# Side matmuls in column tiles, an end stage in halves and other constants in a fused attention kernel's written order

## The chip, the core and the metric

The kernel runs on one core of a Trainium2 chip. The metric is the device time of one execution in microseconds; smaller is better. The engines named below are TensorE (PE in the profile, with PEld for its weight loads), ScalarE (ACT), VectorE (DVE), GpSimd (POOL) and SyncE (SP), whose queue here only starts DMAs.

## What is computed

One block with layer norm, 32-head attention over 2048 tokens of 640 features (20 per head), and a gated linear unit whose output scales the attention's:

```python
def _A_ref(x, wqkv, wo):          # H = 32, Dh = 20
    q, k, v = heads of x @ wqkv
    p = _softmax(einsum("bhqd,bhkd->bhqk", q, k) * Dh ** -0.5)
    return (einsum("bhqk,bhkd->bhqd", p, v) as [B, S, D]) @ wo

def _B_ref(x, w_gate, w_up, w_down):          # F = 1728
    h = _sigmoid(x @ w_gate) * (x @ w_up)
    return h @ w_down

xn = _layernorm(x)
s = _A_ref(xn, A_wqkv, A_wo)
g = _silu(_B_ref(xn, B_w_gate, B_w_up, B_w_down))
return x + s * g
```

The inputs are bf16.

## The kernel before, in words

**Blocks and tiles.** Heads go in 8 groups of 4, queries in 4 chunks of 512: 32 blocks. A block has 64 score tiles of 128 keys by 512 queries, one for each of 16 key tiles and 4 heads. The last two head groups alternate (`gc_of`), so block 30 is group 6 and block 31 group 7 of the last chunk, and blocks 28 and 29 are those of the third.

**The three kinds of TensorE work.** Scores (`score_mm`, L883) use tiles of 32 rows by 128 columns, up to four at a time (one for each head). PV (`pv_emit`, L920) uses tiles of 128 rows by 21 columns at columns 0, 32, 64 and 96, four at a time, which add into one bank, `oacc`. Everything else is a side item: query, key and value projections, gate and up (`mk_gu`, L677), down (`mk_down`, L723) and output rows (`mk_out`, L778). These use the whole array, 128 by 128, except for the bound of the later groups (`mk_bu`, L601), which writes four tiles of 6 columns.

**The exponential is shared.** ScalarE takes two score tiles in one instruction (`pt`) and now and then a third (`px`). VectorE takes one tile at a time out of PSUM as bits (`iv`, L1264) and makes the exponential of four such tiles in three passes (L998, L1001, L1004 into `pb`).

**The order is written out.** A loop with a clock of its own (`now`, in steps of 0.02 us) walks through the work before anything runs and puts each instruction into its engine's program as soon as that engine, a bank and the buffers are free by its table of durations: `T_F`, `T_PV`, `T_MM` 0.2133 us, `T_MODE` 0.107 for a change between kinds, `EL` and `PL` for the way of a result. Each round of scores (`nxt = "F"`) fills one half of ScalarE's PSUM (`scA`) and perhaps a bank more for ScalarE and one for VectorE. `URGENT`, `WAIT3`, `DQ`, `STARVE` decide when a round comes and how many tiles it takes; `D_LAST_END` is the number of tiles left in the last block at which VectorE takes no more. The chip then runs each engine's program in that order and waits on semaphores.

**Normalization of a block.** `norm_a` copies `oacc` to `on` and sends the denominators through DRAM into `lt`; 6.5 us later by the table `norm_b` takes the reciprocal (L959) and sends it back, spread over rows, as `rl`. From 7.2 us after that GpSimd multiplies in four parts (L969), each placed by `beat` behind a PSUM read of VectorE. `norm_c` then starts four or five copies into `oU` at once (L988). `o_at[b]`, 4.8 us later, opens what reads them: the output rows of a chunk wait for the block in `need` (block 29 for the third chunk, eight items).

**The end.** When the last PV is out, `chain` takes block 31 another way: two copies of `oacc` (`e_on`, L1036), transposes (L1040), division (`div_scale`, L751 and L753), transposes back (L1050) and copies into `oU` (L1053). The last chunk's product with `wo` is made in advance for the four row tiles of features that don't need block 31: `fill` holds one matmul of 512 columns (`mains`) and one of 128 (`rest`) per row tile and feature tile `kd` 0 to 3 (L1025). `kd` 3 needs block 30. Those in banks 0 to 2 start only once no item is left and at most `FILL_AT` tiles are unclaimed. The fifth feature tile (`late_mm`, L1029) and the elementwise work and output (`tail_steps`, L1077 to L1102) come after `chain`.

Of the kernel before, what the change touches and what calls it, by code (L numbers as in the profile page):

```python
# [18 lines left out]
P = 128  # L19
# [32 lines left out]
def kernel(  # L52
# [393 lines left out]
    T_IV, T_ON = 0.605, 0.60  # L446
    T_PASS = (0.1333, 0.1333, 0.27)
# [21 lines left out]

    class Item:  # L470
        def __init__(self, ops, at, need=None, pre=(), gates=None):
# [26 lines left out]
    def k_mm1(ps, g, c, kd):  # L498
        nc.tensor.matmul(ps, lhsT=wslice(g, 1, kd), rhs=xnT[:, c, kd, :],
                         start=(kd == 0), stop=(kd == KD - 1))  # L500

    def mk_q(b, at):
# [6 lines left out]
        def mm(kd):  # L509
            nc.tensor.matmul(st["ps"], lhsT=wslice(g, 0, kd), rhs=xnT[:, c, kd, :],  # L510
                             start=(kd == 0), stop=(kd == KD - 1))
# [4 lines left out]
        def ev():  # L516
# [3 lines left out]
                     ("PE", None, [(T_MM, lambda: q_bound(st["ps"], g, st["aq"]))]),  # L520
# [14 lines left out]
    def u_mm(st, u, i, c, kd):  # L535
        nc.tensor.matmul(st["ps"], lhsT=wus[u][:, kd, i, :], rhs=xnT[:, c, kd, :],  # L536
                         start=(kd == 0), stop=(kd == KD - 1))

    def mk_ku(u, c, at):
# [5 lines left out]
        def ev():  # L545
            st["k"] = wk.tile([P, QC], BF16, tag="ku", bufs=2, name="ku")[0:UC, :]
# [26 lines left out]
    def mk_qu(u, c, at):  # L573
# [10 lines left out]
        def ev():  # L584
            st["q"] = wk.tile([P, QC], BF16, tag="ku", bufs=2, name="qu")[0:UC, :]
# [7 lines left out]
    def mk_bu(u, at):  # L593
# [10 lines left out]
        def ev():  # L604
            bt = wk.tile([P, QC], BF16, tag="ku", bufs=2, name="bt")
# [4 lines left out]
        return Item([("PE", alloc, [(T_MM + 2 * T_MODE, mm)]),  # L610
# [30 lines left out]
    def mk_v(pr, tts, at):  # L641
# [10 lines left out]
        def done(t):  # L652
            for tt in tts:
                v_at[(pr, tt)] = t
        return Item([("PE", alloc, [(0.08, lambda i=i, kd=kd: mm(i, kd)) for i in range(len(tts)) for kd in range(KD)]),
                     ("DVE", 0.065 + 0.167 * len(tts), lambda: v_evac(st["ps"], pr, tts), "free", done)], at)

    def mk_gu(c, kf, at):
# [16 lines left out]
        def mm(key, i, kd):  # L675
            w = wgu_tiles[(c, k2)]
            nc.tensor.matmul(st[key][0:fs, :], lhsT=w[:, i, kd, ko * P:ko * P + fs],  # L677
                             rhs=xnT[:, c, kd, :], start=(kd == 0), stop=(kd == KD - 1))
# [9 lines left out]
        def mm2(kd):  # L688
            nc.tensor.matmul(st["g"], lhsT=wgu_tiles[(c, k2)][:, 0, kd, P:2 * P],
                             rhs=xnT[:, c, kd, :], start=(kd == 0), stop=(kd == KD - 1))  # L690
# [24 lines left out]
    def mk_down(c, t4, h, at):  # L715
# [6 lines left out]
        def mm(kf):  # L722
            nc.tensor.matmul(st["ps"][:, 0:HD], lhsT=hT[:, kf, t4 * P:(t4 + 1) * P],  # L723
                             rhs=wd[:, kf, h * HD:(h + 1) * HD],
                             start=(kf == 0), stop=(kf == NFT - 1))
# [40 lines left out]
    def mk_out(tt, h, at):  # L766
# [9 lines left out]
        def mm(kd):  # L776
            hs = slice(h * HD, (h + 1) * HD)
            nc.tensor.matmul(st["ps"][:, 0:HD], lhsT=oU[:, kd, tt * P:(tt + 1) * P], rhs=wo[:, kd, hs],  # L778
                             start=(kd == 0), stop=(kd == KD - 1))
# [176 lines left out]
    def norm_b(b, on, lt):  # L956
# [10 lines left out]
        def part(i):  # L967
            cs = slice(i * P, (i + 1) * P)
            ins = nc.gpsimd.tensor_tensor(out=on_bf[:, cs], in0=on[:, cs], in1=rl[:, cs], op=ALU.mult)  # L969
            if i == QC // P - 1:  # L970
                norm_c(b, on_bf)
                o_at[b] = now + 4.8
            return ins
        for i in range(QC // P):
            pool_q.append((now + 7.2, "n", lambda i=i: part(i)))

    def norm_c(b, on_bf):
        g, c = gc_of(b)
        for j in range(GH):
# [3 lines left out]
            while left:  # L983
# [4 lines left out]
                nc.sync.dma_start(out=oU[o:o + m, t, c * QC:(c + 1) * QC], in_=on_bf[r:r + m, :])  # L988
                f += m
                r += m  # L990
                left -= m

# [27 lines left out]
    mains = [scA[1][:, 0, :], scA[1][:, 1, :], bank[0], bank[1]]  # L1020
# [13 lines left out]
    def e_on(i):  # L1034
        last["on", i] = w2.tile([P, QC], FP32, tag="on", bufs=2, name="on")[:, 0:HQ]
# [16 lines left out]
    def e_o(i):  # L1052
        nc.vector.tensor_copy(out=oU[0:GC, KD - 1, c0 + i * HQ:c0 + (i + 1) * HQ], in_=last["t", i][0:GC, 0:HQ])  # L1053

    chain = [("DVE", 0.34, lambda: e_on(0), ()), ("DVE", 0.34, lambda: e_on(1), ()),
             ("PE", 0.40, lambda: e_tr(0), (0,)), ("PE", 0.40, lambda: e_tr(1), (1,)),
             ("DVE", 0.50, lambda: e_scale(0), (2, 3)), ("DVE", 0.50, lambda: e_scale(1), (2, 3)),
             ("PE", 0.25, lambda: e_back(0), (4,)), ("PE", 0.25, lambda: e_back(1), (4, 5)),
             ("DVE", 0.27, lambda: e_o(0), (6,)), ("DVE", 0.27, lambda: e_o(1), (7,))]
    chain_end = {}  # L1060

    def chain_next(eng):
        k = next((k for k, x in enumerate(chain) if x[0] == eng and k not in chain_end), None)
        return k if k is not None and all(chain_end.get(d, 1e9) <= now for d in chain[k][3]) else None

    def chain_run(k):
# [4 lines left out]
    fill = [(t4 - 2, 0.2133, lambda t4=t4, kd=kd: early(mains[t4], t4, slice(0, 512), kd))  # L1071
            for t4 in (2, 3, 0, 1) for kd in range(KD - 1)]
    fill[2 * (KD - 1):2 * (KD - 1)] = [
        (2, 0.07, lambda t4=t4, kd=kd: early(rest[:, t4 * EX:(t4 + 1) * EX], t4, slice(512, D), kd, t4 == 0))
        for t4 in range(4) for kd in range(KD - 1)]

    def tail_steps():  # L1077
        tmps = [hfl[:, t4 * 2 * D:t4 * 2 * D + 1024].bitcast(FP32) for t4 in range(4)]
        xg = xl.rearrange("p (t u) -> p t u", u=D)
        tmp = hfl[:, 8 * D:8 * D + 8 * EX].bitcast(FP32).rearrange("p (t e) -> p t e", e=EX)  # L1080
# [384 lines left out]
```

## Time and profile before

| | us |
|---|---|
| median of 3 runs | 814.01 |
| lowest and highest | 813.37, 815.41 |
| profiled execution, its own time | 813.36 |
| its span, first to last instruction | 811.6 |
| TensorE, VectorE, ScalarE busy | 776.3, 774.6, 780.8 |
| GpSimd busy | 107.7 |
| HBM traffic over the span | 69 GB/s |

A row of the page gives line, engine, operation, output and input, shape and count, then busy time, the mean of one in ns, and the idle time before. A row of the timeline gives start and duration in us. Several matmuls of one group start within some ns of each other and each is listed with its own full latency, so what a group costs is read from start to start, not from its duration. The granted TensorE clock is 0.995 over the span.

### The profile page before, as it was taken

What the parts mean: (1) busy time and instruction counts of PE and PEld (TensorE: products, weight loads), DVE (VectorE), ACT (ScalarE), POOL (GpSimd) and SP (SyncE); (2) the same over time, 40 slices, a digit from 0 to 9 for tenths busy, and PEclk for the clock granted to TensorE, in tenths of its full rate; (3) what the DMA queues carried; (4) which work ended last, traced back from release to release, by engine and by line L of the source; (5) the groups of instructions that cost most, each with busy time, mean ns of one, the idle gap of its engine ahead of it and who ended that gap; (6) DMA issues with size and microseconds to landing.
All of it is one profiled execution on the core that took longest, in us unless ns stands there. A gap on an engine that the chain in (4) does not pass through costs nothing. (4 is left out here: it accounts for less than half of the span.)

```text
span 811.6 us, 17415 instructions
## 1 busy us (share of the span) xinstructions
PE 776.3 (96%) x6480; PEld 273.2 (34%) x6480; DVE 774.6 (95%) x1248; ACT 780.8 (96%) x991; POOL 107.7 (13%) x225
## 2 busy tenths in 40 slices
PE   7899999999999999999999999999999999999995
PEld 5522222333333323333333222333333223333332
DVE  7799999999999999999999999999999999999995
ACT  8899999999999999999999999999999999999991
POOL 7200000000010000000000000000100203203124
PEclk9999999999999999999999999999999999999998
DMA  5531211123222223212112131232222232312211
GB/s 160 156 103 50 66 52 40 59 58 96 63 70 69 68 58 85 66 55 61 55 58 67 51 100 54 71 104 81 63 70 60 72 88 67 123 57 82 83 52 61
DMA packets 91797, 59.96 MB, mean 74 GB/s; under 512 B 34868, under 2 KB 85604, under 8 KB 91712
## 3 DMA queue, kind: packets, MB, share of 16 engines
q1 hardware_dynamic: 91424, 58.52, 25.8%
q8 instruction: 51, 0.84, 0.4%
q14 instruction: 34, 0.28, 0.1%
q10 hardware_dynamic: 288, 0.33, 0.1%
HBM read 45.18 MB, written 11.09 MB: 69 GB/s over the span
## 5 line engine op out<-in xcount | busy, mean ns | idle before, releaser
L82 ACT ACTIVATE pt<-scA 128x1024 bf16<-128x1024 f32 x704 | 694.7, 1142 | 4.1 <-PE bk L883 3.1
L1264 DVE TENSOR_SCALAR iv<-bk 128x512 int16<-128x512 f32 x504 | 333.6, 681 | 10.2 <-PE bk L883 9.0
L883 PE MATMUL scA<-q,kT 32*128 32x512 bf16 x1401 | 273.1, 382 | 12.9 <-ACT pt L82 7.7
L883 PE MATMUL bk<-q,kT 32*128 32x512 bf16 x647 | 207.4, 383 | 0.1
L920 PE MATMUL oacc<-pt,v 128*21 128x512 bf16 x1401 | 179.4, 382 | 0.6 <-DVE on L949 0.6
L883 PEld LDWEIGHTS <-kT 32*128 32x128 bf16 x2048 | 84.1, 91 | 260.5 <-issue 249.6
L920 PE MATMUL oacc<-pb,v 128*21 128x512 bf16 x1008 | 159.7, 382 | 0.8 <-DVE pb L1004 0.7
L1004 DVE TENSOR_TENSOR pb<-iv,pb 128x2048 bf16<-128x2048 bf16 x126 | 153.9, 1221 | 1.0
L677 PE MATMUL bk<-xnT,wgu 128*128 128x512 bf16 x520 | 148.0, 383 | 1.6 <-DVE iv L1264 0.7
L969 POOL TENSOR_TENSOR on_bf<-on,rl 128x128 bf16<-128x128 f32 x124 | 59.3, 481 | 636.2 <-DVE pb L1004 160.1
L82 ACT ACTIVATE px<-bk 128x512 bf16<-128x512 f32 x143 | 100.5, 717 | 2.7 <-POOL hT L1113 1.6
L998 DVE TENSOR_SCALAR pb<-iv 128x2048 int16<-128x2048 int16 x126 | 86.3, 685 | 0.9
L1001 DVE TENSOR_SCALAR pb<-iv 128x2048 int16<-128x2048 int16 x126 | 86.9, 690 | 0.1
L723 PE MATMUL bk<-wd,hT 128*128 128x320 bf16 x448 | 83.8, 302 | 2.2 <-DVE iv L1264 1.4
L920 PEld LDWEIGHTS <-v 128*21 128x21 bf16 x2552 | 49.4, 91 | 86.4 <-issue 63.5
L677 PEld LDWEIGHTS <-wgu 128*128 128x128 bf16 x520 | 38.2, 97 | 67.6 <-issue 47.9
L920 PE MATMUL oacc<-px,v 128*21 128x512 bf16 x143 | 49.0, 382 | 0.0
L723 PEld LDWEIGHTS <-hT 128*128 128x128 bf16 x448 | 34.6, 97 | 41.4 <-issue 33.8
L536 PE MATMUL bk<-xnT,wu 128*128 128x512 bf16 x160 | 47.3, 383 | 1.2 <-DVE qu L586 1.0
L82 ACT ACTIVATE tnh<-bk 128x512 bf16<-128x512 f32 (+1 forms) x56 | 39.7, 709 | 0.1
L685 DVE SCALAR_TENSOR_TENSOR hT<-tnh,bk 128x512 bf16<-128x512 bf16 x52 | 35.3, 679 | 1.4 <-PE bk L677 0.7
L794 POOL TENSOR_TENSOR xnT<-otmp,xnT 128x160 bf16<-128x160 f32 x48 | 26.2, 567 | 47.9 <-DVE pb L1001 15.6
(111 smaller groups left out, 408.2 us busy)
## 6 DMA issues: line engine op xcount, KB each, us to landing
rl<-rd SPq DMA_DIRECT2D x124, 64.0 KB
wgu<-in_B_w_gate_dram SPq DMA_DIRECT2D x24, 320.0 KB
wgu<-in_B_w_up_dram SPq DMA_DIRECT2D x24, 320.0 KB
gq_dram<-gqs SPq DMA_DIRECT2D x24, 160.0 KB
xnT<-gq_dram SPq DMA_DIRECT2D x12, 320.0 KB
xt<-in_A_x_dram SPq DMA_DIRECT2D x16, 160.0 KB
xnT<-in_A_x_dram SPq DMA_DIRECT2D x16, 160.0 KB
out_dram<-xnT SPq DMA_DIRECT2D x14, 160.0 KB
```

The source lines that it names most:

```text
L82: return nc.scalar.add_instruction(mybir.InstActivation(func=func, name=nc.get_next_instruction_name(), engine=ENG.Activation, ins=[nc.sca ...
L536: nc.tensor.matmul(st["ps"], lhsT=wus[u][:, kd, i, :], rhs=xnT[:, c, kd, :], start=(kd == 0), stop=(kd == KD - 1))
L677: nc.tensor.matmul(st[key][0:fs, :], lhsT=w[:, i, kd, ko * P:ko * P + fs], rhs=xnT[:, c, kd, :], start=(kd == 0), stop=(kd == KD - 1))
L685: return nc.vector.scalar_tensor_tensor(out=hT[0:fs, kf, :], in0=st["t"][0:fs, :], scalar=1.0, in1=st["u"][0:fs, :], op0=ALU.add, op1=ALU. ...
L723: nc.tensor.matmul(st["ps"][:, 0:HD], lhsT=hT[:, kf, t4 * P:(t4 + 1) * P], rhs=wd[:, kf, h * HD:(h + 1) * HD], start=(kf == 0), stop=(kf = ...
L883: nc.tensor.matmul(dst, lhsT=kTs[gc_of(b)[0] % 2][32 * j:32 * j + 32, kt * P:(kt + 1) * P], rhs=qts[b % 3][32 * j:32 * j + 32, :], start=T ...
L920: nc.tensor.matmul(oacc[32 * j:32 * j + DH + 1, :], lhsT=lhsT, rhs=u["src"], start=first, stop=last, tile_position=(0, 32 * j), skip_group ...
L969: ins = nc.gpsimd.tensor_tensor(out=on_bf[:, cs], in0=on[:, cs], in1=rl[:, cs], op=ALU.mult)
L998: ins = nc.vector.tensor_scalar(out=pb[:, 0, :, :].bitcast(I16), in0=iv, scalar1=0x7F80, scalar2=1, op0=ALU.bitwise_and, op1=ALU.bitwise_or)
L1001: ins = nc.vector.tensor_scalar(out=pb[:, 1, :, :].bitcast(I16), in0=iv, scalar1=0x007F, scalar2=0x3F00, op0=ALU.bitwise_and, op1=ALU.bitw ...
L1004: ins = nc.vector.tensor_tensor(out=pb[:, 1, :, :], in0=iv.bitcast(BF16), in1=pb[:, 1, :, :], op=ALU.mult)
L1264: beat(nc.vector.tensor_scalar(out=d["iv"][:, j, :], in0=bank[bk], scalar1=B_OFF, scalar2=0.0, op0=ALU.add, op1=ALU.max))
```

## The change

- All side matmuls except those of the value projection go through `cols`: four matmuls of 32 columns of weights, at PV's four column positions, in place of one of 128. The order's table counts PV and these as one family (`FAM`), the value projection and the end's matmuls as another (`full`, "W").
- The bound item is counted without its two changes.
- `norm_b` comes 9.0 us after `norm_a` (`T_LT`) for all blocks but block 30, which keeps 6.5.
- Block 30's multiply is one instruction (`whole`), placed 6.5 us after its reciprocal, not behind reads of VectorE. In the last block `beat` also lets other GpSimd work go that is 1 us late (`LATE`).
- The copies into `oU` are started 1.5 us apart (`T_OU`) for all blocks but the last two, and `o_at` is later by as much.
- The end: the two copies of `oacc` share one buffer; banks 0 and 1 serve row tiles 0 and 1, `scA[1]` row tiles 2 and 3; `kd` 3 waits for block 30 by the table, the others don't; the late matmuls, elementwise work and output become steps of `chain` in two halves, so the second half's transposes can lie beside the first half's work. The sequence of elementwise steps on VectorE stays.
- `ku` gets a third buffer. `URGENT` 0.15 to 0.2, `D_LAST_END` 12 to 20, `WAIT3` 0 to 0.2, `DQ` 1.0 to 1.4, `STARVE` 0.2 to 0.3, `FILL_AT` 24 to 40.

```diff
-URGENT, ROUNDS, HOLD, SLACK, LEAD, LAG, D_LAST, D_LAST_END = 0.15, 6, 0.0, 0.0, 40.0, 2.0, 20, 12
-M_ORD, WAIT3, FALL, M_END = 1, 0.0, 1, 2.0
+URGENT, ROUNDS, HOLD, SLACK, LEAD, LAG, D_LAST, D_LAST_END = 0.2, 6, 0.0, 0.0, 40.0, 2.0, 20, 20
+M_ORD, WAIT3, FALL, M_END = 1, 0.2, 1, 2.0
...
-XMAX, DQ, DORD, XORD, STARVE = 2, 1.0, 2, 0, 0.2
+XMAX, DQ, DORD, XORD, STARVE = 2, 1.4, 2, 0, 0.3
-FILL_AT = 24
+FILL_AT = 40
...
+    LATE, T_LT, T_OU = 1.0, 9.0, 1.5
...
+    def cols(out, lhsT, rhs, start, stop):
+        for j in range(0, P, 32):
+            nc.tensor.matmul(out[j:j + 32, :], lhsT=lhsT[:, j:j + 32], rhs=rhs, start=start, stop=stop,
+                             tile_position=(0, j), skip_group_check=True)
+
+    FAM = {"F": 0, "PV": 1, "M": 1, "W": 2, None: 3}
...
-            nc.tensor.matmul(st["ps"][:, 0:HD], lhsT=hT[:, kf, t4 * P:(t4 + 1) * P],
-                             rhs=wd[:, kf, h * HD:(h + 1) * HD],
-                             start=(kf == 0), stop=(kf == NFT - 1))
+            cols(st["ps"][:, 0:HD], hT[:, kf, t4 * P:(t4 + 1) * P], wd[:, kf, h * HD:(h + 1) * HD],
+                 kf == 0, kf == NFT - 1)
...
-        if psum and prev is not None and x is not None and pool_at[0] <= now + 0.1:
+        if x is not None and base() == NBLK - 1 and x[0] + LATE <= now and pool_at[0] <= now:
+            pool_q.remove(x)
+            x[2]()
+            pool_at[0] = now + 0.5
+        elif psum and prev is not None and x is not None and pool_at[0] <= now + 0.1:
...
+        def whole():
+            nc.gpsimd.tensor_tensor(out=on_bf, in0=on, in1=rl, op=ALU.mult)
+            norm_c(b, on_bf)
+        if b == NBLK - 2:
+            timed.append((now + 6.5, whole))
+            return
...
-                nc.sync.dma_start(out=oU[o:o + m, t, c * QC:(c + 1) * QC], in_=on_bf[r:r + m, :])
+                parts.append((oU[o:o + m, t, c * QC:(c + 1) * QC], on_bf[r:r + m, :]))
...
+        for i, (o, x) in enumerate(parts):
+            if b < NBLK - 2:
+                timed.append((now + T_OU * i, lambda o=o, x=x: nc.sync.dma_start(out=o, in_=x)))
+            else:
+                nc.sync.dma_start(out=o, in_=x)
+        o_at[b] = now + 4.8 + (T_OU * (len(parts) - 1) if b < NBLK - 2 else 0.0)
...
-    mains = [scA[1][:, 0, :], scA[1][:, 1, :], bank[0], bank[1]]
+    mains = [bank[0], bank[1], scA[1][:, 0, :], scA[1][:, 1, :]]
...
     def e_on(i):
-        last["on", i] = w2.tile([P, QC], FP32, tag="on", bufs=2, name="on")[:, 0:HQ]
+        if i == 0:
+            last["on"] = w2.tile([P, QC], FP32, tag="on", bufs=2, name="on")
+        last["on", i] = last["on"][:, i * HQ:(i + 1) * HQ]
...
              ("DVE", 0.27, lambda: e_o(0), (6,)), ("DVE", 0.27, lambda: e_o(1), (7,)),
+             ("PE", 0.54, lambda: e_late(0), (8,), (0, 1)),
+             ("DVE", 0.63, lambda: t_main(0), (10,)), ("DVE", 0.63, lambda: t_main(1), (10,)),
+             ("DVE", 0.9, lambda: t_done(0), (10,)),
+             ("PE", 0.54, lambda: e_late(1), (9,), (0, 1, 2, 3)),
+             ("DVE", 0.63, lambda: t_main(2), (14,)), ("DVE", 0.63, lambda: t_main(3), (14,)),
+             ("DVE", 1.6, lambda: t_done(1), (14,))]
...
+    fill = fills(lambda t: t, (0, 1), pre, *main) + fills(lambda t: 2, (0, 1), pre, *narrow)
+    fill += fills(lambda t: t, (0, 1), [KD - 2], *main) + fills(lambda t: 2, (0, 1), [KD - 2], *narrow)
+    fill += fills(lambda t: t + 1, (2, 3), pre, *main) + fills(lambda t: 2, (2, 3), pre, *narrow)
+    fill += fills(lambda t: t + 1, (2, 3), [KD - 2], *main) + fills(lambda t: 2, (2, 3), [KD - 2], *narrow)
...
+            if kd == KD - 2 and o_at.get(NBLK - 2, 1e9) > now:
+                return False
...
-                        end = now + T_F + (T_MODE if mode != "F" else 0.0)
+                        end = now + T_F + (T_MODE if fam != "F" else 0.0)
...
-                    dur = T_PV + (T_MODE if mode != "PV" else 0.0)
+                    dur = T_PV + (T_MODE if FAM[fam] != 1 else 0.0)
```

`t_main`, `t_rest`, `t_last` and `t_out` hold the elementwise work and the output DMAs of the former `tail_steps`, cut by row tile; `e_late` holds its late matmuls.

More of the change, by code (lines that the diff above doesn't have):

```diff
@@ L498, in k_mm1 @@
     def k_mm1(ps, g, c, kd):
-        nc.tensor.matmul(ps, lhsT=wslice(g, 1, kd), rhs=xnT[:, c, kd, :],
-                         start=(kd == 0), stop=(kd == KD - 1))
+        cols(ps, wslice(g, 1, kd), xnT[:, c, kd, :], kd == 0, kd == KD - 1)
     def mk_q(b, at):
@@ L509, in mm @@
         def mm(kd):
[L510 to L511 removed]
+            cols(st["ps"], wslice(g, 0, kd), xnT[:, c, kd, :], kd == 0, kd == KD - 1)
         def ab():
@@ L978, in norm_c @@
         g, c = gc_of(b)
+        parts = []
         for j in range(GH):
@@ L1063, in chain_next @@
         k = next((k for k, x in enumerate(chain) if x[0] == eng and k not in chain_end), None)
-        return k if k is not None and all(chain_end.get(d, 1e9) <= now for d in chain[k][3]) else None
+        return k if k is not None and all(chain_end.get(d, 1e9) <= now for d in chain[k][3]) and (
+            len(chain[k]) < 5 or not any(x[4] in chain[k][4] for x in fill)) else None
     def chain_run(k):
```

150 lines of the change are left out of this document (80 added, 70 removed).

## The prediction, made before the changed kernel was run

> **What bounds the kernel now.** I read the page's totals first, then the window from 40 to 780 us (the part in which all engines run), then the waits.
>
> ```profile
> PE 776.3 (96%) x6480; PEld 273.2 (34%) x6480; DVE 774.6 (95%) x1248; ACT 780.8 (96%) x991; POOL 107.7 (13%) x225
> ...
> 40.00:780.00 740.00, 721.47 (x6006) 241.74 (x6005) 721.57 (x1135) 734.74 (x914) 75.05 (x152) 1.00 0.25 70
> ...
> PE scA L883 <- ACT pt L82: 7.7, 28, 0.9
> ```
>
> In those 740 us TensorE (first number) is idle for 18.5 us, VectorE for 18.4, ScalarE for 5.3, at a granted clock of 1.00. No engine alone is the bound: each waits a little for the others in the order that was written out (the last line: 28 waits of TensorE for ScalarE's exponentials, 7.7 us). ScalarE has least room, so it caps what a faster TensorE can give. Outside the window lies an end in which nearly nothing overlaps; it is taken apart below.
>
> **Column tiles: the drain.** TensorE's own time is not all streaming. Its timeline at 400 us, with the weight loads of the three PV groups last:
>
> ```profile
> 399.99 0.31 PE L723 MATMUL bk<-wd,hT 128*128 128x320 bf16 x1
> 400.23 0.39 PE L920 MATMUL oacc<-pb,v 128*21 128x512 bf16 x3
> ...
> 401.37 0.40 PE L920 MATMUL oacc<-pb,v 128*21 128x512 bf16 x4
> ...
> 401.80 0.39 PE L920 MATMUL oacc<-pb,v 128*21 128x512 bf16 x4
> 402.13 0.39 PE L883 MATMUL scA<-q,kT 32*128 32x512 bf16 x2
> ...
> 402.48 0.70 PE L723 MATMUL bk<-wd,hT 128*128 128x320 bf16 x4
> ...
> 401.36 0.33 PEld L920 LDWEIGHTS <-v 128*21 128x21 bf16 x12 [0.28 <-issue]
> ```
>
> Four 320-wide matmuls take 0.70 us, the last of them 0.30 (the mean on this line), so one follows another after (0.70-0.30)/3 = 0.133 us. From such a matmul to the first PV group it is 400.23-399.99 = 0.24: the change of shape costs 0.107. PV to PV is 0.215 (401.37 to 401.80 over two groups; the line left out is the middle one), PV to scores 0.33, so about 0.11 there too. Do equal column tiles avoid it? One operation of before is already in column tiles of another width, the bound of the later head groups:
>
> ```profile
> 269.67 0.39 PE L920 MATMUL oacc<-pb,v 128*21 128x512 bf16 x3
> 269.88 0.39 PE L601 MATMUL bk<-aq,mdu 120*6 120x512 bf16 x4
> 270.21 0.60 PE L677 MATMUL bk<-xnT,wgu 128*128 128x512 bf16 x2
> ```
>
> PV to L601 takes 0.21, a plain group; L601 to the full 128*128 tile takes 0.33. So column tiles of 6 and 21 columns share a shape, and I take it that 32 does too.
>
> How often is it saved? Along TensorE's timeline between 22 and 794 us side matmuls that will be column tiles and PV meet 95 times, the first and last here:
>
> ```profile
> 37.74 0.39 PE L920 MATMUL oacc<-pt,v 128*21 128x512 bf16 x3
> ...
> 38.07 0.60 PE L499 MATMUL bk<-xnT,wqk 128*128 128x512 bf16 x2
> ...
> 792.00 0.84 PE L778 MATMUL bk<-wo,oU 128*128 128x320 bf16 x5
> 792.78 0.40 PE L920 MATMUL oacc<-pb,v 128*21 128x512 bf16 x4
> ```
>
> That is 95 x 0.107 = 10.2 us of TensorE's time. The value matmuls stay whole, so their 5 meetings with other side matmuls now cost a drain: -0.5, leaving 9.7. The far more frequent changes to and from scores stay. What follows of 9.7 in the span? Below: nothing, if ScalarE paces. Above: all of it, and some more if the new constants join more score tiles in one round (WAIT3 waits 0.2 us for a bank, DQ admits more VectorE tiles); each round saved is worth two drains and a 0.213 stream, 0.43, so twenty of them 8.6. I take **5 us**, because the row nearest to the answer is ScalarE's idle 5.3 in the window: what it cannot absorb must move to VectorE, in batches of four.
>
> **Column tiles: their own cost.** Each whole matmul becomes four, with four loads.
>
> ```profile
> L677 PE MATMUL bk<-xnT,wgu 128*128 128x512 bf16 x520 | 148.0, 383 | 1.6 <-DVE iv L1264 0.7 <-DVE kT L152 0.4
> L723 PE MATMUL bk<-wd,hT 128*128 128x320 bf16 x448 | 83.8, 302 | 2.2 <-DVE iv L1264 1.4 <-ACT px L82 0.4 <-DVE ku L547 0.2
> L778 PE MATMUL bk<-wo,oU 128*128 128x320 bf16 x120 | 22.3, 301 | 0.2
> L920 PEld LDWEIGHTS <-v 128*21 128x21 bf16 x2552 | 49.4, 91 | 86.4 <-issue 63.5
> ```
>
> For 512 columns PV is the price: 0.215 a group, as much as the planner's 0.2133 for a whole one, and its loads end early: twelve of them lie in 0.33 us from 401.36, all over before the third group starts at 401.80. Cost: nothing. The 448+120 = 568 groups of 320 columns have no such row. From below nothing: a load of 91 ns is shorter than the 133 ns stream that covers it. From above all of the load laid bare, 0.091 x 568 = 52 us of TensorE. I take nothing, since a load that starts with the group before is done in time; half of the upper end, 26, is the slower rival.
>
> The Trainium skill, "TensorEngine Tiling (Array Packing)", Restrictions and Gotchas, says that column tiling excludes Fast Weight Load, which speaks against this change. By the formula in "TensorE: Matmul & The Clock Gate", LDWEIGHTS (columns over 1.2 GHz), 32 columns take an estimated 27 ns, four in turn 107; by that the sum stays as it is, by bare loads it grows. No run here shows it for 320 columns.
>
> **The end.** From the last block's predecessor (block 30) to the first DVE step of the end stage (L1088):
>
> ```profile
> 783.58 0.24 DVE L959 RECIPROCAL rt<-lt 128x16 f32<-128x16 f32 x1
> ...
> 794.05 1.70 POOL L969 TENSOR_TENSOR on_bf<-on,rl 128x128 bf16<-128x128 f32 x4 [1.95 <-issue]
> 794.63 0.42 DVE L1036 COPY on<-oacc 128x256 f32<-128x256 f32 x1 [0.31 <-PE oacc L920]
> 795.77 3.79 SPq L988 DMA_DIRECT2D oU<-on_bf  x5
> 795.78 0.42 DVE L1036 COPY on<-oacc 128x256 f32<-128x256 f32 x1 [0.73 <-POOL on_bf L969]
> 796.54 0.30 PE L778 MATMUL bk<-wo,oU 128*128 128x320 bf16 x1
> 798.54 0.39 PE L1025 MATMUL bk<-wo,oU 128*128 128x512 bf16 x1 [1.05 <-DMA oU<-on_bf]
> 799.08 0.32 DVE L753 TENSOR_TENSOR onq<-scA,rq 128x160 bf16<-128x160 f32 x1 [1.60 <-PE tp L1050]
> 799.60 1.70 PE L1025 MATMUL bk<-wo,oU 128*128 128x512 bf16 x19
> ...
> 799.72 0.47 DVE L1053 COPY oU<-tp 80x256 bf16<-80x256 bf16 x2
> ...
> 801.14 1.89 PE L1025 MATMUL scA<-wo,oU 128*128 128x512 bf16 x8
> ...
> 802.87 0.59 PE L1029 MATMUL scA<-wo,oU 128*128 128x512 bf16 x2
> ...
> 803.57 0.69 DVE L1088 SCALAR_TENSOR_TENSOR hT<-scA,gql 128x512 f32<-128x512 f32 x1 [3.38 <-PE scA L1029]
> ```
>
> Block 30's multiply on POOL ran only when it was flushed at 794.05, so its copies to oU land late, and the partial output matmuls (L1025) stand behind them in TensorE's order, then the transposes behind those. New: the multiply comes 6.5 us after the reciprocal, 783.6+6.5 = 790.1, in one instruction of about 1.7 us; five copies issued over 3.8 us follow, the last issued at 795.6. Before, L1025's wait for the copies ended at 798.54, 2.8 us after the first was issued; so the last one is in by about 798. The second on copy no longer takes a buffer that POOL reads (0.73), and the second scaling no longer stands behind L1025 (1.60). From the first on copy to the end of the last copy into oU (L1053) it took 800.19-794.63 = 5.56; less 0.73 and 1.60 it is 3.23, to 797.86. The late matmuls take 0.70 (802.87 to 803.57), so L1088 could begin at 798.6, 5.0 us earlier.
>
> What is late instead are the output rows of the third quarter:
>
> ```profile
> 774.48 0.46 POOL L969 TENSOR_TENSOR on_bf<-on,rl 128x128 bf16<-128x128 f32 x1 [0.74 <-DVE pb L998]
> ...
> 779.67 0.84 PE L778 MATMUL bk<-wo,oU 128*128 128x320 bf16 x5
> ```
>
> They open 4.8 us after block 29's last multiply, 774.48+4.8 = 779.3, and their matmuls do start at 779.67. With the reciprocal 2.5 later and four copies 1.5 apart (+4.5) the planner opens them up to 7 us later, near 786, and the partial sums in banks 0 to 2 may start only when all eight are issued. From 779.67 to 796.54 they took 2.1 us each beside the scores; from 786 to 792 three fit, and the other five, at 0.8 each on an idle TensorE (0.70 and a change), end at 796. So they end about where they did, and then remain 8 main (0.215) and 8 narrow matmuls (16+3 of both kinds took 1.70: about 0.06), 2.2 us, to 798.7, and the late ones, 0.7: L1088 at **799.4, 4 us earlier**. The bounds: 5.0 earlier, and 2.1 later (rows at 2.1 each to the end, 786+8x2.1 = 802.8, then 2.2 and 0.7, 805.7). From L1088 on DVE's order is the same, 8.0 us to the end, so the two halves as such gain nothing more: DVE is their chain.
>
> **The rest at nothing.** The spread copies free SP (3.8 us in one piece above), which hides them; they delay only the row gate just priced. The third ku buffer and VectorE's earlier stop (two tiles more for ScalarE, at most 0.57 each by half of its 1142 ns) lie within 1 us either way.
>
> ```profile
> L82 ACT ACTIVATE pt<-scA 128x1024 bf16<-128x1024 f32 x704 | 694.7, 1142 | 4.1 <-PE bk L883 3.1 <-PE scA L883 0.5
> ```
>
> **Sum.** The profiled execution took 813.36 us; -5 and -4 give 804.4. The median of the runs, 814.01, is 0.65 above that execution; I hand in 804.5.
>
> **The rivals.** (a) ScalarE paces, or 32 and 21 columns don't share a shape: the 5 are not gained, 809.4. For it: ScalarE idles for 5.3 us only; against it: VectorE has 18.4 and the split between the two is free, and the 6-column tile beside PV drained nothing. (b) Output rows keep their 2.1 us and L1088 comes 2.1 later: 813.4-5+2.1 = 810.5. For it: the gate moves by 7 us; against: TensorE and the banks are free by then. (c) The new order joins more rounds and both gains come whole: -9.7, -3 (a third of the twenty rounds) and -5.0, 795.7. Against: 18.4 us of VectorE are all there is to take it up. (d) Loads bare in the 320-wide groups: half the upper bound, 26 us of TensorE, less the 9.7 and the end's 4, is 12.3 more: 825.7. It decides from (9.7+4)/568 = 24 ns a group. Against it: loads of 91 ns under a stream of 133. (e) The written order no longer matches the engines' true pace and gives back what is won: 813.
>
> **Chances.** Forecast 0.42 (its own range 801 to 808), (a) 0.20, (b) 0.13, (c) 0.11, (d) 0.08, (e) 0.06. A measurement of this kernel tells about 0.3%, 2.4 us, from no change: faster are the forecast, (a), (b), (c), 0.86; the same (e), 0.06; slower (d), 0.08. The range from 797 to 812 holds the forecast, (a), (b), and part of (c).
>
> **What would show it.** Right: PV to a side matmul at 0.215 with no 0.107 between, 320-wide groups at 0.133 to 0.147, POOL's on_bf of block 30 before 792, no wait on DMA at L1025, and the span from the last PV to L1088 near 5 us instead of 9. Wrong: 320-wide groups above 0.16, side matmuls 0.32 from PV, the last L778 after 798, or ScalarE's idle unchanged while TensorE's grows.

## The result, and the profile after

| | us |
|---|---|
| before, median of 6 runs | 813.96 (812.82 to 816.15) |
| after, median of 6 runs | 806.72 (806.26 to 809.05) |
| ratio, 95% interval | 0.9911 (0.9893 to 0.9928) |
| after, profiled execution, and its span | 806.3, 804.6 |

The change made the kernel 0.9% faster. Predicted were 804.5 us, range 797 to 812. The two profiles split the gain at the last PV, the first step of the elementwise work (L1088 before, L1086 after) and the end of the program:

| us | before | after | predicted |
|---|---|---|---|
| last PV starts | 794.20 | 788.10 | 5 earlier |
| from there to the first elementwise step | 9.37 | 7.13 | 5.2 (799.4-794.2) |
| from there to the end of the span | 8.03 | 9.37 | as before |

So 6.1 us came before the last PV, and 0.9 in the end stage instead of 4. Of the 6.1, 0.3 were there before the first exponential of score tiles starts (30.79 before, 30.46 after). That is the start of the executions and not the change: in the fourteen traces it lies between 30.43 and 31.70. The page's totals, then the window from 40 to 780 us (busy time of TensorE, weight loads, VectorE, ScalarE, GpSimd, then the granted clock), then the wait of TensorE for the exponentials (us, times, longest):

```profile
PE 776.9 (97%) x10462; PEld 285.5 (35%) x10466; DVE 770.8 (96%) x1241; ACT 780.2 (97%) x990; POOL 106.4 (13%) x222
```

```profile
40.00:780.00 740.00, 728.12 (x9945) 254.98 (x9937) 724.74 (x1140) 739.43 (x919) 74.13 (x154) 1.00 0.26 70
```

```profile
PE scA L885 <- ACT pt L82: 5.1, 17, 0.9
```

ScalarE is idle for 740-739.43 = 0.6 us of these 740, where it was 5.3 before. After the change ScalarE sets the pace there. As long as it keeps its share of the exponential, nothing that frees another engine can gain more in this stretch. TensorE's busy time over the span, 776.9 against 776.3, does not show the drains, since a matmul's own latency of 0.3 to 0.4 us covers a gap of 0.1; they are read from start to start.

The tiles, on TensorE's timeline:

```profile
776.60 0.32 PE L473 MATMUL bk<-wo,oU 128*32 128x320 bf16 x4
776.74 0.38 PE L922 MATMUL oacc<-pt,v 128*21 128x512 bf16 x2
...
780.28 0.86 PE L473 MATMUL bk<-wo,oU 128*32 128x320 bf16 x20
```

From a 320-wide group to PV is now 0.14, where it was 0.24. Five such groups (twenty matmuls) take 0.86 us and the last of them 0.30, so one follows another after 0.56/4 = 0.14, as the whole ones did. Over all pairs of groups from 22 us to the last PV the median from a 512-wide side group to PV went from 0.319 to 0.227, from PV to a side group from 0.328 to 0.223.

The end:

```profile
777.45 0.24 DVE L965 RECIPROCAL rt<-lt 128x16 f32<-128x16 f32 x1
...
783.25 3.25 POOL L796 TENSOR_TENSOR xnT<-otmp,xnT 128x160 bf16<-128x160 f32 x4 [0.78 <-POOL xnT L796]
...
786.47 1.27 POOL L980 TENSOR_TENSOR on_bf<-on,rl 128x512 bf16<-128x512 f32 x1
787.77 3.78 SPq L1008 DMA_DIRECT2D oU<-on_bf  x5
...
788.52 0.76 DVE L1056 COPY on<-oacc 128x256 f32<-128x256 f32 x2
...
789.82 0.32 PE L473 MATMUL bk<-wo,oU 128*32 128x320 bf16 x4
790.23 0.33 DVE L756 TENSOR_TENSOR onq<-scA,rq 128x160 bf16<-128x160 f32 x1
...
792.98 0.33 DVE L756 TENSOR_TENSOR onq<-scA,rq 128x160 bf16<-128x160 f32 x1 [2.31 <-DMA oU<-on_bf]
...
795.23 1.29 DVE L1086 SCALAR_TENSOR_TENSOR hT<-bk,gql 128x512 f32<-128x512 f32 x2 [1.14 <-PE bk L1047]
...
796.97 0.42 DVE L1092 SCALAR_TENSOR_TENSOR hT<-bk,gql 128x256 f32<-128x256 f32 x1 [0.45 <-PE bk L1043]
797.42 1.19 DVE L1096 TENSOR_TENSOR xnT<-hT,xnT 128x256 bf16<-128x256 f32 x1
797.44 0.38 PE L1043 MATMUL bk<-wo,oU 128*128 128x128 bf16 x4 [0.52 <-DVE hT L1092]
```

Block 30's multiply now runs before the last PV, and the last output row (L473 with `wo`) ends at 790. But the multiply comes 786.47-777.45 = 9.0 us after its reciprocal, not 6.5, since GpSimd is at the additions of the output rows (L796) until 786.5. Its copies are issued 0.3 us ahead of the last PV, where 2.4 were forecast (791.8 and 794.2). And the second scaling waits 2.31 us for a DMA: `onq` is allocated under the tag `on_bf`, which has two buffers, and the second `onq` gets the one that block 30's five copies still read. Everything behind it on VectorE, the transposes and the elementwise work, waits with it. In the elementwise part the halves now get in each other's way. VectorE waits 0.45 us for narrow partial sums and TensorE 0.52 us for VectorE, since both halves share the bank of the narrow ones, and an addition (L1096) takes 1.19 us, where this line took 0.55 and 0.84 before.

### The profile page after: what moved, and what is told of

The parts are those of the page before. It is cut to its first block, busy times and chain, and to the rows that moved or that the text cites. A ratio compares the mean times of both kernels' runs of the same rounds, so it can differ in the third digit from the quotient of the medians.

```text
span 804.6 us, 25389 instructions
## 1 busy us (share of the span) xinstructions
PE 776.9 (97%) x10462; PEld 285.5 (35%) x10466; DVE 770.8 (96%) x1241; ACT 780.2 (97%) x990; POOL 106.4 (13%) x222
## 4 chain that ended last, share of the span: by engine, by line
ACT 44%; PE 42%; issue 6%; DVE 4%; POOL 1%; SPq 1%; DMA 1%; DVEq 0%; ACTq 0%; POOLq 0%
ACT pt L82 35%; PE bk L473 18%; PE scA L885 13%; PE oacc L922 8%; ACT px L82 5%; ACT tnh L82 2%; DVE iv L1316 2%; ACT td L82 1%; DVE pb L1022 1%; PE bk L885 1%; POOL xnT L796 1%; PE tp L292 1%; DVE pb L1019 1%; ACT aq L173 0%; PE psk L142 0%
## 5 line engine op out<-in xcount | busy, mean ns | idle before, releaser
L82 ACT ACTIVATE pt<-scA 128x1024 bf16<-128x1024 f32 x706 | 707.5, 1196 | 0.5 <-PE bk L885 0.2
L1316 DVE TENSOR_SCALAR iv<-bk 128x512 int16<-128x512 f32 x500 | 332.0, 680 | 12.6 <-PE bk L885 9.9
L885 PEld LDWEIGHTS <-kT 32*128 32x128 bf16 x2048 | 89.4, 91 | 262.7 <-issue 251.1
L473 PE MATMUL bk<-xnT,wgu 128*32 128x512 bf16 x2160 | 157.3, 383 | 0.5 <-DVE iv L1316 0.2
L82 ACT ACTIVATE px<-bk 128x512 bf16<-128x512 f32 x140 | 104.6, 764 | 1.8 <-POOL hT L1158 1.6
L473 PE MATMUL bk<-wd,hT 128*32 128x320 bf16 x1792 | 86.7, 302 | 0.1
L922 PEld LDWEIGHTS <-v 128*21 128x21 bf16 x2548 | 54.1, 91 | 77.3 <-issue 55.1
L473 PEld LDWEIGHTS <-wgu 128*32 128x32 bf16 x2160 | 44.5, 95 | 64.3 <-issue 46.3
L473 PEld LDWEIGHTS <-hT 128*32 128x32 bf16 x1792 | 37.1, 95 | 37.6 <-issue 31.9
L473 PE MATMUL bk<-xnT,wu 128*32 128x512 bf16 x640 | 48.5, 384 | 0.6 <-DVE iv L1316 0.2
L82 ACT ACTIVATE tnh<-bk 128x512 bf16<-128x512 f32 (+1 forms) x56 | 43.4, 775 | 0.1
L796 POOL TENSOR_TENSOR xnT<-otmp,xnT 128x160 bf16<-128x160 f32 x48 | 27.1, 584 | 57.4 <-DVE otmp L791 16.2
```

Of the source, the lines that this page charges most:

```text
L82: return nc.scalar.add_instruction(mybir.InstActivation(func=func, name=nc.get_next_instruction_name(), engine=ENG.Activation, ins=[nc.sca ...
L473: nc.tensor.matmul(out[j:j + 32, :], lhsT=lhsT[:, j:j + 32], rhs=rhs, start=start, stop=stop, tile_position=(0, j), skip_group_check=True)
L796: add = nc.gpsimd.tensor_tensor(out=xr[:, cs], in0=tmp[:, i * HD // 2:(i + 1) * HD // 2], in1=xr[:, cs], op=ALU.add)
L885: nc.tensor.matmul(dst, lhsT=kTs[gc_of(b)[0] % 2][32 * j:32 * j + 32, kt * P:(kt + 1) * P], rhs=qts[b % 3][32 * j:32 * j + 32, :], start=T ...
L922: nc.tensor.matmul(oacc[32 * j:32 * j + DH + 1, :], lhsT=lhsT, rhs=u["src"], start=first, stop=last, tile_position=(0, 32 * j), skip_group ...
L1316: beat(nc.vector.tensor_scalar(out=d["iv"][:, j, :], in0=bank[bk], scalar1=B_OFF, scalar2=0.0, op0=ALU.add, op1=ALU.max))
```

## The experiments

The kernel before, run beside them on the same three chips, had medians of 814.16 to 814.5; ratios are to it. "ScalarE idle" is 740 us less its busy time in the window from 40 to 780, "waits for `lt`" those of VectorE's reciprocal (L959 before, L965 after) over the whole run, and "last PV" its start in the profiled execution.

| kernel | us, median | ratio, interval | ScalarE idle | waits for `lt` | last PV |
|---|---|---|---|---|---|
| before | 814.16 to 814.5 | | 5.3 | 3.3 in 4 | 794.20 |
| after | 806.72 | 0.9911 (0.9893 to 0.9928) | 0.6 | none | 788.10 |
| tiles in the old order | 820.38 | 1.0077 (1.0046 to 1.0108) | 10.1 | 6.7 in 5 | 799.31 |
| whole matmuls in the new order | 807.09 | 0.9906 (0.9878 to 0.9934) | 0.9 | none | 789.63 |
| new constants alone | 811.70 | 0.9963 (0.9950 to 0.9977) | 3.0 | 2.2 in 2 | 792.23 |
| new order, old constants | 805.22 | 0.9885 (0.9853 to 0.9917) | 0.9 | none | 788.59 |
| both normalization times as before | 812.19 | 0.9973 (0.9945 to 1.0000) | 5.0 | 6.5 in 4 | 795.36 |
| normalization times alone | 813.55 | 0.9979 (0.9965 to 0.9993) | 3.2 | none | 794.88 |
| reciprocal early, copies spread | 813.60 | 0.9986 (0.9968 to 1.0003) | 4.9 | 6.8 in 5 | 798.49 |
| reciprocal at 10 | 809.82 | 0.9937 (0.9917 to 0.9957) | 1.9 | 3.1 in 1 | 795.65 |
| drains in the table | 810.25 | 0.9936 (0.9915 to 0.9957) | 3.5 | none | 791.75 |
| drains in the table, reciprocal at 10 | 809.93 | 0.9939 (0.9921 to 0.9957) | 2.2 | none | 793.68 |
| `onq` in buffers of its own | 804.79 | 0.9870 (0.9848 to 0.9892) | 0.6 | none | 789.36 |
| the same, old constants, narrow sums ahead | 805.53 | 0.9883 (0.9862 to 0.9904) | 0.9 | none | 788.50 |

### Is it the tiles?

Two kernels part the instructions from the order: the kernel before with every side matmul in column tiles and its order untouched, and the kernel after with its order and every one of these matmuls whole.

```diff
-        nc.tensor.matmul(ps, lhsT=wslice(g, 1, kd), rhs=xnT[:, c, kd, :],
-                         start=(kd == 0), stop=(kd == KD - 1))
+        cols(ps, wslice(g, 1, kd), xnT[:, c, kd, :], kd == 0, kd == KD - 1)
...
```

> The kernel before with its side matmuls (all but the values') split into four column tiles, the written order untouched. Theory A, that the time up to the last PV is won by the drains saved between side matmuls and PV: the order of before has 95 such meetings, 0.10 us each, about 10 us of TensorE, of which some 5 reach the end; last PV near 789 instead of 794.2, time 808 to 811. Rival B, that the new constants of the order win it: within 2 us of 814. Rival D, that column tiles cost something in themselves: each of the about 400 changes from a side matmul to scores 10 ns longer, 4 us, so that little is left, 812 to 814.

```diff
-        for j in range(0, P, 32):
-            nc.tensor.matmul(out[j:j + 32, :], lhsT=lhsT[:, j:j + 32], rhs=rhs, start=start, stop=stop,
-                             tile_position=(0, j), skip_group_check=True)
+        nc.tensor.matmul(out, lhsT=lhsT, rhs=rhs, start=start, stop=stop, skip_group_check=True)
```

> The changed kernel with whole 128-column side matmuls again, in the same written order. Theory A: the new order has about 128 meetings of side matmuls and PV, each with a drain of 0.10 us again, 12.8 us of TensorE, of which 6 to 10 reach the end: 813 to 817. Rival B (constants): within 2 us of 806.7. Rival D: the 10 ns at each change to scores come back as a gain of 4 us against 12.8, so 811 to 813.

The whole matmuls in the new order pay each drain again. Their timeline, a 320-wide one and PV behind it:

```profile
401.19 0.31 PE L472 MATMUL bk<-wd,hT 128*128 128x320 bf16 x1
401.43 0.39 PE L920 MATMUL oacc<-pb,v 128*21 128x512 bf16 x1
```

That is 0.24 again, and at 126 meetings, more than the 92 of before, because this order is made for free changes: 126 x 0.107 = 13.5 us of TensorE. (The prediction's 95 has three meetings with the bound's 6 columns in it, which paid no drain.) Still the time is 807.09, with an interval that covers that of the kernel after. With the two sequences of ScalarE's instructions laid side by side it is 1.0 us later at the end of the steady part, and 0.3 of that was there at 12 us, before the first of these matmuls. So the tiles themselves are worth some 0.7 us here, and the order nearly all of the steady gain; the expectation had put 6 to 10 us on the tiles.

The tiles in the old order are slower than before, by 6.2 us, which none of the three expectations held. Laid side by side with the kernel before, instruction for instruction of ScalarE, they are 0.3 us ahead at 13 us, before any of these matmuls, and 0.1 ahead at 280 us, although by then 33 drains are saved (3.5 us of TensorE). So the drains gave ScalarE nothing there. Then 2.7 us are lost at 333 to 338, 0.9 near 641 and 2.1 at 716 to 724. The end loses 3.5 more in the profiled execution: the first elementwise step comes 812.16-799.31 = 12.85 after the last PV, the second scaling waits 3.52 for block 30's copies, and the granted clock is 0.5 from 806.3 to 809.8. At the first of the three places before the end the queue of SP, VectorE and TensorE show:

```profile
322.51 3.08 SPq L986 DMA_DIRECT2D oU<-on_bf  x4
325.70 0.53 SPq L949 DMA_DIRECT2D ld<-on  x1
...
327.42 0.35 SPq L951 DMA_DIRECT2D lt<-ld  x1
...
331.69 0.25 DVE L957 RECIPROCAL rt<-lt 128x16 f32<-128x16 f32 x1 [2.06 <-DMA lt<-ld]
...
334.40 0.37 PE L881 MATMUL bk<-q,kT 32*128 32x512 bf16 x1 [0.71 <-DVE iv L1262]
...
335.57 1.90 PE L472 MATMUL bk<-xnT,wgu 128*32 128x512 bf16 x16 [0.23 <-DVE iv L1262]
...
338.11 1.02 ACT L82 ACTIVATE pt<-scA 128x1024 bf16<-128x1024 f32 x1 [1.79 <-PE bk L881]
```

The first DMA with the denominators (`ld`) stands behind four copies of the block before into `oU`, which occupy the queue for 3.08 us. The way back (`lt`) is issued at 327.42 and ends the wait at 331.69, 4.3 us later. The kernel before has the same four copies ahead of it, and there the same step took 2.4:

```profile
323.43 3.10 SPq L988 DMA_DIRECT2D oU<-on_bf  x4
326.63 0.53 SPq L951 DMA_DIRECT2D ld<-on  x1
...
328.33 0.35 SPq L953 DMA_DIRECT2D lt<-ld  x1
...
330.75 0.25 DVE L959 RECIPROCAL rt<-lt 128x16 f32<-128x16 f32 x1 [0.89 <-DMA lt<-ld]
```

VectorE sits 2.06 us in front of the reciprocal, the score tiles behind it are read late, TensorE waits for them (0.71) and ScalarE for TensorE (1.79). So the reciprocal, 6.5 us after its copy by the table, is at the edge of the way through DRAM and back. Why the way back took 4.3 and 2.4 was not tried, but the DMA records differ. In the slower one, a view of the DMAs from 327 to 332 has a transfer that the other kernel lacks from 328 to 331, one of 16 KB of the kind `instruction` (queue and kind, then packets, MB, share of 16 engines' time):

```profile
q8 instruction: 1, 0.02, 1.7%
```

Of the 434 transfers of this step in all fourteen traces, 102 have such a 16 KB transfer in their first 1.5 us. They land 2.4 us after their issue at the median, the others after 1.7. The two go together in the records; no run tests whether one causes the other.

### Which part of the order?

Eight kernels take parts of the new order away or put them alone into the old one. The third `ku` buffer, `LATE` and block 30's single multiply had no kernel of their own. First the scheduling constants, alone in the kernel before, and taken back in the kernel after:

```diff
-URGENT, ROUNDS, HOLD, SLACK, LEAD, LAG, D_LAST, D_LAST_END = 0.15, 6, 0.0, 0.0, 40.0, 2.0, 20, 12
-M_ORD, WAIT3, FALL, M_END = 1, 0.0, 1, 2.0
+URGENT, ROUNDS, HOLD, SLACK, LEAD, LAG, D_LAST, D_LAST_END = 0.2, 6, 0.0, 0.0, 40.0, 2.0, 20, 20
+M_ORD, WAIT3, FALL, M_END = 1, 0.2, 1, 2.0
...
-XMAX, DQ, DORD, XORD, STARVE = 2, 1.0, 2, 0, 0.2
+XMAX, DQ, DORD, XORD, STARVE = 2, 1.4, 2, 0, 0.3
...
-FILL_AT = 24
+FILL_AT = 40
```

> The kernel before with the new constants of the order alone (URGENT, D_LAST_END, WAIT3, DQ, STARVE, FILL_AT). Theory A: 814 within 2 us. Rival B: 5 to 7 us faster, 807 to 809.

> The changed kernel with the old constants of the order. Theory A: 805 to 809, the column tiles keep the gain. Rival B: 811 to 814.

Alone they give 2.5 us, between the two expectations; taken back from the kernel after, they cost nothing (805.22 against 806.72). They are not what the gain hangs on.

Then the times of the normalization, taken back in the kernel after, and put alone into the kernel before:

```diff
-    LATE, T_LT, T_OU = 1.0, 9.0, 1.5
+    LATE, T_LT, T_OU = 1.0, 6.5, 0.0
```

> The changed kernel with the reciprocal again 6.5 us after the copy of the sums and the copies into oU in one piece. Theory C, formed after the first four runs: the time up to the last PV is won by the later reciprocal and the spread copies, since VectorE no longer waits for lt (3.3 us in four waits before, each stopping TensorE and ScalarE behind it, none after): some such waits come back, ScalarE idles 3 to 6 us again, last PV 791 to 794, time 810 to 813. Rival F, that the order's table without drains between side matmuls and PV wins it: within 2 us of 806.7.

> The kernel before with the later reciprocal (9.0 us but for block 30) and the spread copies alone. Theory C: no wait of VectorE for lt, last PV 789 to 791, 808 to 811 (the end stage as before). Rival F: within 2 us of 814.

Without them the kernel after falls back to 812.19, and the waits for `lt` are there. Alone in the kernel before they remove its waits for `lt` entirely and give 0.9 us only, none of it ahead of the last PV (794.88 against 794.20); 808 to 811 was expected. So they are needed but not enough. The next kernel tells the two apart: the copies stay spread, and only the reciprocal is early again. The one after it sets the reciprocal later still.

```diff
-    LATE, T_LT, T_OU = 1.0, 9.0, 1.5
+    LATE, T_LT, T_OU = 1.0, 6.5, 1.5
```

> The changed kernel with the reciprocal again 6.5 us after the copy of the sums; the copies into oU stay spread. If the reciprocal's time is the part of theory C that counts: VectorE waits for lt again (some us in all), 809 to 813. If the spread of the copies counts: within 2 us of 806.7.

```diff
-    LATE, T_LT, T_OU = 1.0, 9.0, 1.5
+    LATE, T_LT, T_OU = 1.0, 10.0, 1.5
```

> The changed kernel with the reciprocal at 10.0 in place of 9.0, a change that should matter to nothing but the order that comes out. If the gain belongs to the table without drains and the late reciprocal: within 2 us of 806.7, ScalarE idle under 1.5 us between 40 and 780. If the changed kernel's order is a lucky draw: 809 to 812, ScalarE idle 3 us or more.

The early reciprocal alone takes nearly the whole gain away (813.60). Up to the last PV it takes more: 798.49 is 4.3 us later than before, with 6.8 us of waits and 6.83 us at half the granted clock from 778.5. The end stage is 3.0 us shorter than in the kernel after and hides part of that (the first elementwise step comes 802.60-798.49 = 4.11 after the last PV). The queue of SP ahead of one of its waits shows why spreading by the table doesn't help:

```profile
750.85 3.02 SPq L1006 DMA_DIRECT2D oU<-on_bf  x4
...
754.49 0.55 SPq L957 DMA_DIRECT2D ld<-on  x1
...
756.95 0.38 SPq L959 DMA_DIRECT2D lt<-ld  x1
...
759.93 0.25 DVE L965 RECIPROCAL rt<-lt 128x16 f32<-128x16 f32 x1 [2.16 <-DMA lt<-ld]
```

The four copies left the queue in one piece all the same, 1.5 us apart by the table and 0.75 apart in fact. The kernel after hardly spreads them either: of its 109 gaps between copies of one block the median is 0.78 us (0.77 before), and 20 are above 1.2. What helps is that VectorE comes to the reciprocal after the data.

At 10 us the time is not that of 9 but 809.82. Block 30, which keeps 6.5 in all these kernels, has its wait here, behind four copies once more:

```profile
775.34 3.03 SPq L1006 DMA_DIRECT2D oU<-on_bf  x4
778.47 0.53 SPq L957 DMA_DIRECT2D ld<-on  x1
...
780.18 0.33 SPq L959 DMA_DIRECT2D lt<-ld  x1
...
783.07 0.25 DVE L965 RECIPROCAL rt<-lt 128x16 f32<-128x16 f32 x1 [3.08 <-DMA lt<-ld]
```

and the window right behind it, with the granted clock third from the end:

```profile
784.00:791.00 7.00, 6.38 (x87) 2.29 (x86) 6.25 (x11) 4.20 (x6) 3.69 (x6) 0.76 0.39 109
```

The wait of 3.1, the stretch of lower clock right behind it (7 x 0.24 = 1.7) and 1.3 more idle time of ScalarE are 6.1 of the 7.5 us by which its last PV is later; 0.9 more were there when the exponentials began (31.38 against 30.46).

Last the table's drains: the kernel after with column tiles, planned as if a change between them and PV cost 0.107, once with the reciprocal at 9 and once at 10.

```diff
-    FAM = {"F": 0, "PV": 1, "M": 1, "W": 2, None: 3}
+    FAM = {"F": 0, "PV": 1, "M": 2, "W": 2, None: 3}
```

> The changed kernel, its order planned as if side matmuls and PV still cost a drain; on the chip they are column tiles. Theory C: within 2 us of 806.7. Rival F: 810 to 814.

> The same 10.0, in the order planned with drains between side matmuls and PV (810.25 at 9.0). If the table counts: 3 us above the run at 10.0 without these drains. If it was a draw: on the same level as that one within 2 us.

At 9 the table with drains is 3.5 us slower than the one without, at 10 the two take the same time (809.93 and 809.82). But the kernel without drains in its table has at 10 the wait and the slow stretch of block 30 just shown, 4.8 us, and the one with them has neither. So without a wait for `lt` the three orders made with drains in the table or with whole matmuls take 809.93, 810.25 and 813.55 (the last with the end stage of before), and the two made for free changes 805.22 and 806.72. That speaks for the table, by some 3 us or more. It is not settled: by what was written down before these runs, equal times at 10 speak for a draw of the order. Each edit makes a wholly new order, five are few, and to take 4.8 from 809.82 is an argument, not a run.

### The end

```diff
-        onq = w2.tile([P, n, GC], BF16, tag="on_bf", bufs=2, name="onq")
+        onq = w2.tile([P, n, GC], BF16, tag="onq", bufs=2, name="onq")
```

> The changed kernel, its last division writing to two buffers of its own instead of those of on_bf; the order is the same. If the wait of 2.31 us before the second division is for the buffer that block 30's copies still read, as the result's trace says, it goes, and the end is then held by the copies themselves (the last lands near 793) and by the partial output matmuls: L1086 1 to 1.5 us earlier, 805 to 806. If the copies hold the late matmuls all the same: 806.7 within 0.4.

```profile
789.36 0.39 PE L922 MATMUL oacc<-pt,v 128*21 128x512 bf16 x2
...
791.43 0.33 DVE L756 TENSOR_TENSOR onq<-scA,rq 128x160 bf16<-128x160 f32 x1
...
791.90 0.33 DVE L756 TENSOR_TENSOR onq<-scA,rq 128x160 bf16<-128x160 f32 x1
...
794.16 0.70 PE L1047 MATMUL bk<-wo,oU 128*128 128x512 bf16 x4 [0.19 <-DMA oU<-on_bf]
794.58 1.29 DVE L1086 SCALAR_TENSOR_TENSOR hT<-bk,gql 128x512 f32<-128x512 f32 x2 [1.56 <-PE bk L1047]
```

The wait is gone, and the first elementwise step comes 794.58-789.36 = 5.22 us after the last PV in place of 7.13. That is the prediction's 5.2, in part by chance: it was made of output rows that end 1.8 us after the last PV and of partial sums right behind them. Here the rows end 2.0 after it, but twelve of the partial sums stand behind the transposes (L1070, 792.38). The median, 804.79, is 1.9 below the 806.72 of the kernel after (measured on another chip; the ratios' intervals just part, 0.9892 and 0.9893). In its trace the last PV is later than in the kernel after only because its start is 1.2 us later (31.70 against 30.46). The kernel with the old constants gets there in another way: its copies are issued earlier, `onq` does not wait, and the first elementwise step comes 793.65-788.59 = 5.06 after the last PV.

```profile
783.00 3.78 SPq L1008 DMA_DIRECT2D oU<-on_bf  x5
...
788.59 0.39 PE L922 MATMUL oacc<-pb,v 128*21 128x512 bf16 x3 [0.54 <-DVE pb L1022]
...
791.19 0.33 DVE L756 TENSOR_TENSOR onq<-scA,rq 128x160 bf16<-128x160 f32 x1
793.65 1.29 DVE L1086 SCALAR_TENSOR_TENSOR hT<-bk,gql 128x512 f32<-128x512 f32 x2 [1.35 <-PE bk L1047]
```

The last kernel joins both and puts the narrow partial sums of the second half ahead in the fill list, against the collision in the shared bank:

```diff
-    fill = fills(lambda t: t, (0, 1), pre, *main) + fills(lambda t: 2, (0, 1), pre, *narrow)
...
+    fill = fills(lambda t: t, (0, 1), pre, *main) + fills(lambda t: 2, (0, 1, 2, 3), pre, *narrow)
...
```

> The version that should beat both: the changed kernel with the old constants (805.2), buffers of its own for the last division, and the second half's narrow partial matmuls ahead of the first half's last ones, so that VectorE's read of the first half's bank does not wait between them. In the run with old constants VectorE waited 0.45 and TensorE 0.52 there, and block 30's copies came early enough, so the buffers give nothing: 804.2 to 805.0. If TensorE alone holds the second half, nothing: 805.2 within 0.5.

```profile
793.90 1.29 DVE L1086 SCALAR_TENSOR_TENSOR hT<-bk,gql 128x512 f32<-128x512 f32 x2 [1.69 <-PE bk L1047]
795.11 0.41 DVE L1092 SCALAR_TENSOR_TENSOR hT<-bk,gql 128x256 f32<-128x256 f32 x1
```

It took 805.53 us (804.06 to 805.65), ratio 0.9883 (0.9862 to 0.9904). VectorE's 0.45 us in front of L1092 and TensorE's 0.52 are gone, and from the first elementwise step to the end of the span it takes 802.2-793.90 = 8.3 us in place of the 9.37 of the kernel after and the 9.3 of the two that it joins (803.0-793.65 and 803.9-794.58): that is what the collision costs. From the last PV to the end are 13.7 us, where the old constants alone had 14.4, but the median shows no gain over them, and 804.2 to 805.0 was expected if it gained. `onq`'s own buffers, the old constants and both together lie within 0.8 us of each other, all below the kernel after; their order can't be told.

## Why the prediction was right, and where it was not

**The total.** 9.5 us were forecast (814.01 to 804.5) and 7.2 came (813.96 to 806.72). The time lies in the range, but partly by luck: the steady part gave more than was forecast, for another cause, and the end stage less.

**The steady part.** 5 us were predicted and 6.1 came. The cap was read rightly: ScalarE's idle 5.3 was what there was to gain in the window, and 4.7 of it were gained. The cause was not: the step that failed is "95 x 0.107 = 10.2 us of TensorE's time" as the source of the 5. The drains did go, each at the price predicted, but TensorE's time was not what ScalarE waited for. The tiles give some 0.7 us in the new order and nothing in the first 280 us of the old. As to the tiles, rival (a), ScalarE paces, was the true one.

What the prediction left out stood in the waits of the profile before:

```profile
DVE rt L959 <- DMA lt<-ld: 3.3, 4, 1.2
```

It costed the later reciprocal by the delay of the output rows alone and the spread copies as freeing SP, "which hides them". But the new order needs the later reciprocal: with the early one VectorE waits for `lt`, the engines behind it stop, and it is back at 813.60. That is not all of it, as the kernel before without these waits gains 0.9 us only, none of it ahead of the last PV. What wins the rest stays open; the table without drains is what the runs point to. "Within 1 us either way" for the constants was too small when they stand alone (2.5), and right in company.

**The column tiles' cost.** Nothing, as predicted: 0.136 at the median for 320 columns, and rival (d), bare loads, is out. "Columns of 6 and 21 share a shape, and I take it that 32 does too" held.

**The end stage.** 4 us were predicted and 0.9 came. The step that failed first is "the second scaling no longer stands behind L1025": it does not, but the same copies hold it through the buffer it writes, 2.31 us. With buffers of its own the predicted 5.2 came. The copies are late, too: "6.5 us after the reciprocal" was 9.0, behind GpSimd's work for the output rows, and where they were issued 5.6 us ahead of the last PV (old constants) the same shared buffer cost no wait. The second failed step is "DVE's order is the same, 8.0 us to the end": the order is, but the halves meet in one bank, and it took 9.37. Together 1.9+1.3 is what lacks to the 4. The signs that were named came (multiply before 792, no wait of L1043 on a DMA), but not the span of 5 us from the last PV (7.13), since none of the others shows the wait that mattered.

**The rows.** The prediction's times are on the clock of the kernel before, so they are compared from the last PV. The rows' matmuls start at 775.47, 12.6 us ahead of it, where the gate at 786 was 8.2 ahead: it was priced 4.4 us too late. The last row ends at 790.1, 2.0 after the last PV, and 796 was 1.8 after it. So the end of the rows was forecast well, rival (b) did not happen, and the gate decided nothing.

**The other rivals.** (c), both gains whole, is out: with ScalarE's idle at 0.6 there was no room for 12.7 us in the steady part. (e), a written order that does not match the true pace, did not happen to the kernel after; the tiles alone in the old order, 6.2 us slower with 6.7 us of waits for `lt`, may be a case of it.

## What to carry to other kernels

A drain saved on an engine that is busy for 97% of the time is worth little as long as another engine paces (some 0.7 of 13.5 us here). Before pricing such a gain, ask which wait of the pacing engine would go. In an order written out by hand look first at the short waits for a DMA on an engine on which the others depend, and at what stands ahead of that transfer in its queue: such an instruction is placed behind the data's latest arrival, not its usual one. Taking such waits out gains only what the rest of the order can use (nothing ahead of the last PV in the kernel before). And a buffer tag shared by two stages is a wait between them: where one stage is moved nearer to the other, look up who reads the buffers that it writes.

## What was not expected of the hardware

**TensorE's clock halves behind short stalls.** After the wait at 331.69 in the tiles in the old order the granted clock is 0.5 for 3.41 us, from 335.3, and again from 721.0, behind the wait that ends at 718.95, and from 806.3 in the end stage. In the first:

```profile
333.00:340.00 7.00, 5.86 (x52) 1.35 (x44) 6.23 (x10) 4.20 (x6) 0.00 (x0) 0.76 0.15 42
```

The mean of 0.76 over 7 us is such a stretch (1-0.5 x 3.41/7). Four 512-wide groups take 1.90 there, 0.425 from one to the next in place of 0.215. So such a stall costs twice, once as a wait and again as a slow stretch. The idle gaps of TensorE before it were below 1 us each (0.71 the longest). A wait for `lt` is not needed for it: the new order with the old constants, one of the fastest, has the clock at 0.5 from 773.5 to 776.9, behind 3.4 us in which TensorE is busy for 2.00 and its longest gap, for ScalarE, is 1.01. No run sets a limit at which it happens. The Trainium skill, "TensorE: Matmul & The Clock Gate", Part 1, has an activity window of 3413 ns and says that short idle times between groups of matmuls can make the clock fall back to half; this trace agrees with the length, 3.41, and with the half.

**The last of four column tiles starts 10 ns after the first, and the change of shape costs what it did.** From the first of four column tiles to scores it took 0.322 us for 512 columns and 0.242 for 320 (the most frequent values), 10 ns more than from whole matmuls (0.312 and 0.232). The four tiles start 3 to 4 ns apart, and from the last of them it is 0.312 and 0.232 again. There are 418 such changes in the kernel after, 4.2 us of TensorE, nearly half of the predicted 9.7; as TensorE does not pace, they cost as little as the drains did.
